# Four alternating layers on one core: PSUM pools of the linear-attention layer split by purpose, small loads and adds moved between engines, weight pieces requested in another order

## The chip, the core and the metric

The kernel runs on one core of a Trainium2 chip. The metric is the device time of one execution in microseconds. Before the change the median of four runs is 8587.26 us (8576.44 to 8593.6).

## What is computed

Four layers run one after the other on x (2048 tokens, 640 features, bf16): A, B, A, B, each as x + layer(layernorm(x)). Layer A is attention in 64 segments of 32 tokens, with 8 memory tokens ahead of each; the first 8 output rows of a segment are the memory of the next, so the segments are a chain. Layer B is linear attention with 32 heads of 20 features:

```
qkv = x @ wqkv                       # 640 -> 3 * 640, 32 heads of 20
pq, pk = q @ w_phi, k @ w_phi        # 20 x 20 for each head
phi_q = concat(softmax(pq), softmax(-pq)); phi_k likewise    # 40 features
kv = sum over s of phi_k * v;  z = sum over s of phi_k
o  = (phi_q @ kv) / (phi_q @ z + 1e-6)
y  = o @ wo
```

## The kernel before

`_layer_a` keeps Wq and Wo in SBUF (16 loads from ScalarE's queue, lines 77 to 82) and streams Wk and Wv anew for each segment: 8 pieces of 960 KB each, into rings of three buffers (`ringk`, `ringv`), requested on SyncE at line 147. A segment projects k and q in three thirds each, then v in three thirds (lines 165 to 169), and goes on to scores, softmax, the product with v and the output projection (lines 176 to 284).

`_layer_b` works in tiles of 128 tokens, 16 in all. Its stages are:

- Start-up: wqkv and wo on SyncE (lines 414 to 417), the 32 blocks of w_phi as 36 small loads on POOL's queue into `wphi_sb` (lines 425 and 427), x into `x_all` (line 472, POOL), layer norm (lines 479 to 489) and transposes into `xnT_all`.
- Key loop (lines 510 to 529): `proj_featT` makes k transposed (25 matmuls, line 504, copied by ScalarE at 506), then v (line 516, copied by VectorE at 518 to 522), then `phi_proj` (lines 447 to 451) and `phi_features` (lines 457 to 466: maximum and minimum, two exponentials on ScalarE, sum, reciprocal, product), which leaves the 40 features per head in `phik_all`.
- Sum over the keys (line 536): 512 matmuls into `kvp`, copied to `kv_sb`.
- Query loop (lines 543 to 583), for each tile: `proj_featT`, `phi_proj`, `phi_features`, 16 transposes (line 553) and a copy of 2048 columns (555), 32 small matmuls with `kv_sb` (560), the scaling by the denominator on VectorE (564 to 568), 5 transposes (572) and a copy (574), 10 matmuls with wo (578), the residual add on VectorE (581, 582) and the store from POOL's queue (583).

The PSUM tiles of projection, v, phi, transposed features, numerators and y all come from one pool, `psG`, with two buffers of two banks each; `phi_features` reads its input from there. SBUF tiles of the two loops come from `tw`, with two buffers for each tag. The framework sets the order of the instructions on each engine beforehand, from the dependences and the pools' buffers; on the chip every engine runs its list in that order, and a wait holds all that stands behind it.

Of the kernel before, what the change touches and what calls it, by code (L numbers as in the profile page):

```python
# [8 lines left out]
BF16 = mybir.dt.bfloat16  # L9
F32 = mybir.dt.float32  # L10
I32 = mybir.dt.int32
ALU = mybir.AluOpType
# [3 lines left out]
P = 128  # L16


def _layer_a(
# [10 lines left out]
    nc = tc.nc  # L30
    S, Dm = x_in.shape
    DC = Dm // P
# [15 lines left out]
    FPV = F // NPIECE_V  # L48
# [3 lines left out]
    ident = gctx["ident"]  # L52
# [4 lines left out]
    wk_v = wk.rearrange("(c p) h e -> p c (h e)", p=P)  # L57
    wv_v = wv.rearrange("(c p) h e -> p c (h e)", p=P)
# [3 lines left out]
    ringk = ctx.enter_context(tc.tile_pool(name="a_ringk", bufs=3))  # L62
    ringv = ctx.enter_context(tc.tile_pool(name="a_ringv", bufs=3))
# [11 lines left out]
    wo_sb = wres.tile([P, FB, Dm], BF16, name="wo_sb")  # L75
# [16 lines left out]
    for ti in range(NT):  # L92
# [7 lines left out]
        for c in range(nchk):  # L100
# [8 lines left out]
                                op0=ALU.subtract, op1=ALU.mult)  # L109
# [11 lines left out]
        for si in range(SPT):  # L121
            s = ti * SPT + si
# [17 lines left out]
            NPK = F // FPV  # L140
            R = 3

            def emit_pieces(wdram_v, ring, tagname, idxs):
                d = {}
                for pi in idxs:
                    pc = ring.tile([P, DC, FPV], BF16, name=f"{tagname}_piece", tag=tagname)
                    nc.sync.dma_start(out=pc[:], in_=wdram_v[:, :, pi * FPV:(pi + 1) * FPV])
# [158 lines left out]
def kernel(  # L306
# [15 lines left out]
    dbg_y: bass.AP | None = None,  # L322
):
    nc = tc.nc
# [9 lines left out]
    gctx = {}  # L334
# [43 lines left out]
def _layer_b(  # L378
# [16 lines left out]
    assert HB * DB == Dm and HB % 2 == 0 and HB * HS == 1024 and DB < HS and FF <= 64  # L395
    NT = S // P
    NPAIR = HB // 2
    HPB = 512 // HS
    eps_t = gctx["eps"]
# [20 lines left out]
    for h in range(HB):  # L420
        r0 = h * DB
        c = r0 // P
        p0 = r0 % P
        n1 = min(DB, P - p0)
        nc.gpsimd.dma_start(out=wphi_sb[p0:p0 + n1, c, h * HS:h * HS + DB], in_=wphi[h, 0:n1, :])
        if n1 < DB:
            nc.gpsimd.dma_start(out=wphi_sb[0:DB - n1, c + 1, h * HS:h * HS + DB], in_=wphi[h, n1:DB, :])

    interior = []
    straddle = []  # L430
    for c in range(DC):
        r_lo, r_hi = c * P, (c + 1) * P
        h_first = -(-r_lo // DB)
        h_last = r_hi // DB - 1
        lo = h_first
        while lo <= h_last:
            hi = min(h_last, (lo // HPB) * HPB + HPB - 1)
            interior.append((c, lo, hi))
            lo = hi + 1
        if r_hi < Dm and r_hi % DB != 0:  # L440
            straddle.append((r_hi // DB, c))

    def phi_proj(ps3, featT_sb):
        flat = ps3[:].rearrange("p h f -> p (h f)")
        for (c, h_lo, h_hi) in interior:
            a, b = h_lo * HS, h_hi * HS + DB
            nc.tensor.matmul(flat[:, a:b], lhsT=featT_sb[:, c, :], rhs=wphi_sb[:, c, a:b], start=True, stop=True)
        for (h, c) in straddle:
            a, b = h * HS, h * HS + DB
            nc.tensor.matmul(flat[:, a:b], lhsT=featT_sb[:, c, :], rhs=wphi_sb[:, c, a:b], start=True, stop=False)  # L450
            nc.tensor.matmul(flat[:, a:b], lhsT=featT_sb[:, c + 1, :], rhs=wphi_sb[:, c + 1, a:b], start=False, stop=True)

    def phi_features(ps3, out_phi):
        pf3 = ps3[:, :, 0:DB]
# [13 lines left out]
                                in1=sm[:].unsqueeze(3).to_broadcast([P, HB, 2, DB]), op=ALU.mult)  # L468

# [30 lines left out]
    def proj_featT(t, col0, dst_sb):  # L500
        ps = psG.tile([P, DC, P], F32, name="b_pT", tag="g")
        for fb in range(DC):
            for c in range(DC):
                nc.tensor.matmul(ps[:, fb, :], lhsT=wqkv_sb[:, c, col0 + fb * P:col0 + (fb + 1) * P],
                                 rhs=xnT_all[:, t * DC + c, :], start=(c == 0), stop=(c == DC - 1))
        nc.scalar.copy(out=dst_sb[:], in_=ps[:])

    hA = 512 // DB
    rem = 512 - hA * DB
    for t in range(NT):  # L510
        kT_sb = tw.tile([P, DC, P], BF16, name="b_kT", tag="featT")
        proj_featT(t, Dm, kT_sb)
        psv = psG.tile([P, 2, 512], F32, name="b_psv", tag="g")
        for c in range(DC):
            for part, (a, b) in enumerate(((0, 512), (512, Dm))):
                nc.tensor.matmul(psv[:, part, 0:b - a], lhsT=xnT_all[:, t * DC + c, :],
                                 rhs=wqkv_sb[:, c, 2 * Dm + a:2 * Dm + b], start=(c == 0), stop=(c == DC - 1))
        nc.vector.tensor_copy(out=v1_all[:, t, 0:hA, 0:DB], in_=psv[:, 0, 0:hA * DB].rearrange("p (h d) -> p h d", d=DB))
        if rem > 0:
            nc.vector.tensor_copy(out=v1_all[:, t, hA, 0:rem], in_=psv[:, 0, hA * DB:512])  # L520
            nc.vector.tensor_copy(out=v1_all[:, t, hA, rem:DB], in_=psv[:, 1, 0:DB - rem])
            nc.vector.tensor_copy(out=v1_all[:, t, hA + 1:HB, 0:DB],
                                  in_=psv[:, 1, DB - rem:Dm - 512].rearrange("p (h d) -> p h d", d=DB))
        else:
            nc.vector.tensor_copy(out=v1_all[:, t, hA:HB, 0:DB],
                                  in_=psv[:, 1, 0:Dm - 512].rearrange("p (h d) -> p h d", d=DB))
        psk = psG.tile([P, HB, HS], F32, name="b_psk", tag="g")
        phi_proj(psk, kT_sb)
        phi_features(psk, phik_all[:, t, :, :])
# [13 lines left out]
    for t in range(NT):  # L543
        qT_sb = tw.tile([P, DC, P], BF16, name="b_qT", tag="featT")
        proj_featT(t, 0, qT_sb)
        psq = psG.tile([P, HB, HS], F32, name="b_psq", tag="g")
        phi_proj(psq, qT_sb)
        phiq = tw.tile([P, NPAIR, 2, 64], BF16, name="b_phiq", tag="phiq")
        nc.vector.memset(phiq[:, :, :, FF:64], 0.0)
        phi_features(psq, phiq[:].rearrange("p j a f -> p (j a) f")[:, :, 0:FF])  # L550
        pqt = psG.tile([P, NPAIR, P], BF16, name="b_pqt", tag="g")
        for j in range(NPAIR):
            nc.tensor.transpose(out=pqt[:, j, :], in_=phiq[:, j, :, :].rearrange("p a f -> p (a f)"), identity=ident[:])  # L553
        phiqT = tw.tile([P, NPAIR, P], BF16, name="b_phiqT", tag="phiqT")
        nc.scalar.copy(out=phiqT[:], in_=pqt[:])  # L555
        psn = psG.tile([P, 2, NPAIR, HS], F32, name="b_psn", tag="g")
        for a in range(2):
            r0 = a * 64
            for j in range(NPAIR):
                nc.tensor.matmul(psn[:, a, j, 0:DB + 1], lhsT=phiqT[r0:r0 + FF, j, :],  # L560
                                 rhs=kv_sb[r0:r0 + FF, j, 0:DB + 1], start=True, stop=True)
        psn_ja = psn[:].rearrange("p a j s -> p j a s")
        rden = tw.tile([P, NPAIR, 2], F32, name="b_rden", tag="rden")
        nc.vector.tensor_scalar(out=rden[:].unsqueeze(3), in0=psn_ja[:, :, :, DB:DB + 1], scalar1=1e-6,
                                scalar2=None, op0=ALU.add)
        nc.vector.reciprocal(out=rden[:], in_=rden[:])
        o_sb = tw.tile([P, Dm], BF16, name="b_o", tag="o")
        nc.vector.tensor_tensor(out=o_sb[:].rearrange("p (j a d) -> p j a d", a=2, d=DB), in0=psn_ja[:, :, :, 0:DB],
                                in1=rden[:].unsqueeze(3).to_broadcast([P, NPAIR, 2, DB]), op=ALU.mult)
# [5 lines left out]
        psy = psG.tile([P, 2, 512], F32, name="b_psy", tag="g")  # L575
        for c in range(DC):
            for part, (a, b) in enumerate(((0, 512), (512, Dm))):
                nc.tensor.matmul(psy[:, part, 0:b - a], lhsT=oT_sb[:, c, :], rhs=wo_sb[:, c, a:b],  # L578
                                 start=(c == 0), stop=(c == DC - 1))
        xo = tw.tile([P, Dm], BF16, name="b_xo", tag="xo")  # L580
        nc.vector.tensor_tensor(out=xo[:, 0:512], in0=x_all[:, t, 0:512], in1=psy[:, 0, 0:512], op=ALU.add)
        nc.vector.tensor_tensor(out=xo[:, 512:Dm], in0=x_all[:, t, 512:Dm], in1=psy[:, 1, 0:Dm - 512], op=ALU.add)
# [36 lines left out]
```

## Time and profile before

| | |
|---|---|
| median of four runs | 8587.26 us |
| profiled execution | 8571.85 us |
| its span | 8570.1 us |
| busy share of PE, PEld, DVE, ACT, POOL | 69%, 62%, 28%, 22%, 1% |
| mean granted TensorE clock | 0.69 |

PE is TensorE's matmuls, PEld its weight loads, DVE is VectorE, ACT is ScalarE, POOL is GpSimd, SP is SyncE. In a row of the timeline stand start, length, engine, line and operation, output and inputs, count, and in brackets how long the engine had been idle and what released it. In a row of costs by line stand the busy time, the mean in ns of one instruction, and the idle time of the engine ahead of it with its releasers. The busy shares are of the whole span, in which layer A has about 87%; what an engine does in layer B is read from windows of that layer.

### The profile page before, as it was taken

The page shows a single profiled execution, that of the slowest core. Times are in us where ns is not written, and L with a number is a line of the kernel's source. Part 1 is how long each engine was busy: PE and PEld are TensorE (multiplying, and loading weights), DVE is VectorE, ACT ScalarE, POOL GpSimd, SP SyncE. Part 2 cuts the span into 40 slices and gives each one's busy share as a digit, 9 for nine tenths or more (in the row PEclk, how much of TensorE's full clock was granted, in tenths as well). Part 3 has the DMA queues.
Part 4 walks back from the last instruction along what each step waited for, and adds up shares of the span by engine and source line. Part 5 has one row for each costly group of instructions (what it writes and reads, how often), then busy time and mean ns, then how long its engine had stood idle before and what let it go on. Part 6 is the DMA issues. An engine that isn't in the chain of part 4 may idle for free.

```text
span 8570.1 us, 324610 instructions
## 1 busy us (share of the span) xinstructions
PE 5916.6 (69%) x156010; PEld 5344.3 (62%) x156010; DVE 2369.8 (28%) x4948; ACT 1854.7 (22%) x2568; POOL 108.4 (1%) x209
## 2 busy tenths in 40 slices
PE   5777777777777777765457777777777777777554
PEld 4666666666666666654346666666666666666543
DVE  2222222222222222235312222222222222222443
ACT  1222222222222222222212222222222222222222
POOL 0000000000000000010000000000000000000100
PEclk7777766766767676666666666667666766766766
DMA  8778778778877877840087787788778787778400
GB/s 306 271 274 281 271 271 286 274 272 279 283 266 275 281 267 272 281 162 6 8 305 271 275 284 271 272 286 284 266 273 289 264 282 270 274 273 280 150 6 8
DMA packets 1381604, 2093.24 MB, mean 244 GB/s; under 512 B 37808, under 2 KB 1376192, under 8 KB 1380288
## 3 DMA queue, kind: packets, MB, share of 16 engines
q1 hardware_dynamic: 1348736, 2019.95, 67.5%
q10 hardware_dynamic: 23040, 31.46, 1.1%
q8 instruction: 1220, 19.99, 1.0%
q0 software_dynamic: 8512, 21.06, 0.8%
q14 instruction: 96, 0.79, 0.0%
HBM read 2061.83 MB, written 10.49 MB: 242 GB/s over the span
## 4 chain that ended last, share of the span: by engine, by line
issue 43%; PE 7%; DVE 2%; DMA 2%; ACT 1%; POOL 0%; POOLq 0%; ACTq 0%
PE p L136 3%; DMA wk_piece<-in_A_Wk_dram 2%; PE y L283 1%; PE vstg L235 1%; DVE v_tok L238 1%; PE po L265 0%; DVE ssb L206 0%; ACT E L210 0%; DVE ssb L204 0%; DVE rmax L208 0%; PE ptp L219 0%; DMA wv_piece<-in_A_Wv_dram 0%; PE b_psy L578 0%; PE b_pqt L553 0%; ACT b_phiqT L555 0%
## 5 line engine op out<-in xcount | busy, mean ns | idle before, releaser
L136 PE MATMUL p<-hT,wv_piece 128*128 128x40 bf16 x30720 | 1120.2, 196 | 486.9 <-DMA wv_piece<-in_A_Wv_dram 362.6
L136 PEld LDWEIGHTS <-wv_piece 128*128 128x128 bf16 x30720 | 1024.8, 107 | 594.4 <-DMA wv_piece<-in_A_Wv_dram 404.7
L136 PE MATMUL p<-hT,wk_piece 128*128 128x40 bf16 x30720 | 1048.6, 188 | 351.4 <-DMA wk_piece<-in_A_Wk_dram 208.4
L136 PE MATMUL p<-hT,wq_sb 128*128 128x40 bf16 x30720 | 1031.5, 190 | 255.0 <-ACT qT_sb L138 122.7
L136 PEld LDWEIGHTS <-wk_piece 128*128 128x128 bf16 x30720 | 942.4, 101 | 387.8 <-DMA wk_piece<-in_A_Wk_dram 231.0
L136 PEld LDWEIGHTS <-wq_sb 128*128 128x128 bf16 x30720 | 969.7, 103 | 304.6 <-issue 294.5
L204 DVE SCALAR_TENSOR_TENSOR ssb<-sA,mask_a 40x640 f32<-40x640 f32 x256 | 210.5, 822 | 2999.4 <-PE sA L182 2995.5
L283 PE MATMUL y<-oT_sb,wo_sb 128*128 128x40 bf16 x30720 | 930.4, 191 | 3.3 <-issue 2.9
L283 PEld LDWEIGHTS <-wo_sb 128*128 128x128 bf16 x30720 | 915.7, 105 | 10.5 <-issue 4.5
L238 DVE COPY v_tok<-vstg 40x1024 bf16<-40x1024 bf16 x768 | 529.1, 689 | 1202.5 <-PE vstg L235 1190.3
L235 PE MATMUL vstg<-ident,vT_sb 128*40 128x128 bf16 x6144 | 700.8, 297 | 212.2 <-ACT vT_sb L138 100.0
L235 PEld LDWEIGHTS <-vT_sb 128*40 128x40 bf16 x6144 | 509.9, 137 | 275.2 <-ACT vT_sb L138 115.2
L138 ACT CAST kT_sb<-p 128x640 bf16<-128x640 f32 x384 | 265.8, 692 | 1641.8 <-PE p L136 1641.8
L138 ACT CAST qT_sb<-p 128x640 bf16<-128x640 f32 x384 | 265.3, 691 | 1352.0 <-PE p L136 1352.0
L265 PE MATMUL po<-PT_sb,v_tok 40*128 40x40 bf16 (+1 forms) x8192 | 335.6, 209 | 298.8 <-DVE v_tok L238 298.8
L265 PEld LDWEIGHTS <-v_tok 40*128 40x128 bf16 (+1 forms) x8192 | 268.0, 124 | 417.7 <-DVE v_tok L238 393.4
L138 ACT CAST vT_sb<-p 128x640 bf16<-128x640 f32 x384 | 265.8, 692 | 1144.4 <-PE p L136 1144.4
L269 ACT CAST oT_sb<-po 128x640 bf16<-128x640 f32 x384 | 265.7, 692 | 615.7 <-PE po L265 597.2
L292 DVE CAST hT<-y 128x8 bf16<-128x8 f32 x640 | 102.8, 161 | 1034.9 <-PE y L283 1034.9
L219 PE MATMUL ptp<-ident,Pn 40*40 40x40 bf16 x4096 | 183.8, 199 | 276.6 <-DVE Pn L213 276.6
L210 ACT ACTIVATE E<-ssb,nrmax 40x640 bf16<-40x640 f32 x256 | 211.2, 825 | 675.8 <-DVE nrmax L209 672.5
L219 PEld LDWEIGHTS <-Pn 40*40 40x40 bf16 x4096 | 154.6, 113 | 297.8 <-DVE Pn L213 291.5
(123 smaller groups left out, 3964.0 us busy)
## 6 DMA issues: line engine op xcount, KB each, us to landing
wk_piece<-in_A_Wk_dram SPq DMA_DIRECT2D x1024, 960.0 KB, 7.9
wv_piece<-in_A_Wv_dram SPq DMA_DIRECT2D x1024, 960.0 KB, 8.3
wq_sb<-in_A_Wq_dram ACTq DMA_DIRECT2D x16, 960.0 KB, 13.3
wo_sb<-in_A_Wo_dram ACTq DMA_DIRECT2D x16, 960.0 KB, 12.7
xscr<-xo_sb POOLq DMA_DIRECT2D x32, 160.0 KB, 2.1
x_all<-xscr POOLq DMA_DIRECT2D x32, 160.0 KB, 5.6
wqkv_sb<-in_B_wqkv_dram SPq DMA_DIRECT2D x6, 800.0 KB, 10.7
x_sb<-in_A_x_dram POOLq DMA_DIRECT2D x16, 160.0 KB, 2.6
```

Of the source, the lines that this page charges most:

```text
L136: nc.tensor.matmul(ps[:, bb, 0:L], lhsT=wb[:, c, :], rhs=hT[:, c, :], start=(c == 0), stop=(c == DC - 1))
L138: nc.scalar.copy(out=dst_sb[:, t3 * 16:(t3 + 1) * 16, :], in_=ps[:, :, 0:L])
L204: nc.vector.scalar_tensor_tensor(out=ssb4, in0=sA[rows, :, :, 0:L], scalar=scale, in1=mask4, op0=ALU.mult, op1=ALU.add)
L210: nc.scalar.activation(out=E[rows], in_=ssb[rows], func=ACT.Exp, bias=nrmax[rows], scale=1.0)
L219: nc.tensor.transpose(out=ptp[r0:r0 + L, g, hid, 0:L], in_=Pn[r0:r0 + L, hid, :], identity=ident[r0:r0 + L, r0:r0 + L])
L235: nc.tensor.transpose(out=stg[g * 64:g * 64 + L, jj, :], in_=vT_sb[:, jg, :], identity=ident[:])
L238: nc.vector.tensor_copy(out=v_tok[g * 64:g * 64 + L, st_i * STG:(st_i + 1) * STG, :], in_=stg[g * 64:g * 64 + L, :, :])
L265: nc.tensor.matmul(po[p0:p0 + sz, bb, 0:L], lhsT=v_tok[r0:r0 + L, jloc, c0:c0 + sz], rhs=PT_sb[r0:r0 + L, hid, :], start=True, stop=True)
L269: nc.scalar.copy(out=oT_sb[:, b_lo:b_lo + 16, :], in_=po[:, :, 0:L])
L283: nc.tensor.matmul(y_ap(c), lhsT=wo_sb[:, k, c * P:(c + 1) * P], rhs=oT_sb[:, k, :], start=(k == 0), stop=(k == FB - 1))
L292: nc.vector.tensor_copy(out=hT_next[:, c, 0:M], in_=y_ap(c)[:, 0:M])
```

## The change

In layer A the eight pieces of Wk are requested ahead of the eight of Wv in the code, where before the first three of each came first. In layer B:

- `psG` is replaced by pools for each purpose: `psP` (projection), `psQ` (phi), `psYV` (v and y), `psQT` (transposed features) with one bank each, `psN` (numerators) with two; `psT` goes from two buffers to one. Work that took two banks at once is done in parts: projection 4 + 1 blocks, phi in two halves of 16 heads, v in 512 + 128 columns one after the other, transposed features in two halves, numerators in four quarters, y in two halves of 320.
- phi is copied by ScalarE to a bf16 tile in SBUF (`pfsb`), and `phi_features` reads that.
- `tw` has three buffers.
- The 36 small loads of w_phi alternate between SyncE and ScalarE.
- The memset of `phiq` moves to GpSimd. y is copied by ScalarE to `ybf`, and GpSimd adds x to it.
- A flag `mimic_b` is passed that nothing reads.

```diff
-            kp = emit_pieces(wk_v, ringk, "wk", range(0, min(R, NPK)))
-            vp = emit_pieces(wv_v, ringv, "wv", range(0, min(R, NPK)))
-            kp.update(emit_pieces(wk_v, ringk, "wk", range(min(R, NPK), NPK)))
-            vp.update(emit_pieces(wv_v, ringv, "wv", range(min(R, NPK), NPK)))
+            kp = emit_pieces(wk_v, ringk, "wk", range(0, NPK))
+            vp = emit_pieces(wv_v, ringv, "wv", range(0, NPK))
...
-    tw = ctx.enter_context(tc.tile_pool(name="b_tw", bufs=2))
+    tw = ctx.enter_context(tc.tile_pool(name="b_tw", bufs=3))
...
-    psG = ctx.enter_context(tc.tile_pool(name="b_psG", bufs=2, space=bass.MemoryType.PSUM))
-    psT = ctx.enter_context(tc.tile_pool(name="b_psT", bufs=2, space=bass.MemoryType.PSUM))
+    psP = ctx.enter_context(tc.tile_pool(name="b_psP", bufs=1, space=bass.MemoryType.PSUM))
+    psQ = ctx.enter_context(tc.tile_pool(name="b_psQ", bufs=1, space=bass.MemoryType.PSUM))
+    psYV = ctx.enter_context(tc.tile_pool(name="b_psYV", bufs=1, space=bass.MemoryType.PSUM))
+    psQT = ctx.enter_context(tc.tile_pool(name="b_psQT", bufs=1, space=bass.MemoryType.PSUM))
+    psN = ctx.enter_context(tc.tile_pool(name="b_psN", bufs=2, space=bass.MemoryType.PSUM))
+    psT = ctx.enter_context(tc.tile_pool(name="b_psT", bufs=1, space=bass.MemoryType.PSUM))
...
-        nc.gpsimd.dma_start(out=wphi_sb[p0:p0 + n1, c, h * HS:h * HS + DB], in_=wphi[h, 0:n1, :])
+        eng = (nc.sync, nc.scalar)[h % 2]
+        eng.dma_start(out=wphi_sb[p0:p0 + n1, c, h * HS:h * HS + DB], in_=wphi[h, 0:n1, :])
...
+    def phi_proj(featT_sb, pfsb):
+        for half in range(2):
+            ps = psQ.tile([P, HH, HS], F32, name="b_psq", tag="q")
...
+            nc.scalar.copy(out=pfsb[:, half * HH:(half + 1) * HH, :], in_=ps[:, :, 0:DB])
...
-        nc.vector.memset(phiq[:, :, :, FF:64], 0.0)
+        nc.gpsimd.memset(phiq[:, :, :, FF:64], 0.0)
...
+        for jr in range(2):
+            pqt = psQT.tile([P, JH, P], BF16, name="b_pqt", tag="qt")
...
+            nc.scalar.copy(out=phiqT[:, jr * JH:(jr + 1) * JH, :], in_=pqt[:])
...
+        for jr in range(2):
+            for a in range(2):
...
+                nc.vector.tensor_scalar(out=rden[:].unsqueeze(2), in0=psn[:, :, DB:DB + 1], scalar1=1e-6,
+                                        scalar2=None, op0=ALU.add)
+                nc.vector.reciprocal(out=rden[:], in_=rden[:])
+                nc.vector.tensor_tensor(out=o4[:, jr * JH:(jr + 1) * JH, a, :], in0=psn[:, :, 0:DB],
+                                        in1=rden[:].unsqueeze(2).to_broadcast([P, JH, DB]), op=ALU.mult)
...
+            nc.scalar.copy(out=ybf[:, a:a + YR], in_=psy[:, 0:YR])
...
-        nc.vector.tensor_tensor(out=xo[:, 0:512], in0=x_all[:, t, 0:512], in1=psy[:, 0, 0:512], op=ALU.add)
-        nc.vector.tensor_tensor(out=xo[:, 512:Dm], in0=x_all[:, t, 512:Dm], in1=psy[:, 1, 0:Dm - 512], op=ALU.add)
+        nc.gpsimd.tensor_tensor(out=xo[:], in0=x_all[:, t, :], in1=ybf[:], op=ALU.add)
```

VectorE in the query loop before, one tile and the start of the next; the number behind a name tells one buffer's use from the next (`b_psn` numerators, `b_o` their scaled values, `b_psy` y, `b_psq` phi):

```order
L564 TENSOR_SCALAR b_rden_85452<-b_psn_85419 128x32
L566 RECIPROCAL b_rden_85452<-b_rden_85452 128x32
L568 TENSOR_TENSOR b_o_85455<-b_psn_85419,b_rden_85452 128x640
L581 TENSOR_TENSOR b_xo_85476<-x_all_82803,b_psy_85465 128x512
L582 TENSOR_TENSOR b_xo_85476<-x_all_82803,b_psy_85465 128x128
L457 TENSOR_REDUCE b_mx_85525<-b_psq_85508 128x1
L458 TENSOR_REDUCE b_mn_85526<-b_psq_85508 128x1
L459 TENSOR_SCALAR b_mx_85525<-b_mx_85525 128x1
L464 TENSOR_REDUCE b_sm_85533<-b_eph_85530 128x64
L465 RECIPROCAL b_sm_85533<-b_sm_85533 128x64
L466 TENSOR_TENSOR b_phiq_85523<-b_eph_85530,b_sm_85533 128x32x40
```

A tile's features (457 to 466) stand behind the last step of the tile before it. VectorE in the same loop now, in the same names (`b_pqsb` is the bf16 copy of phi); from one tile to the next the number of a name grows by 163:

```order
L592 TENSOR_TENSOR b_o_85844<-b_psn_85884,b_rden_85893 128x8x20
L473 TENSOR_SCALAR b_mx_86137<-b_mx_86137 128x1
L471 TENSOR_REDUCE b_mx_86300<-b_pqsb_86279 128x1
L472 TENSOR_REDUCE b_mn_86301<-b_pqsb_86279 128x1
L473 TENSOR_SCALAR b_mx_86300<-b_mx_86300 128x1
L478 TENSOR_REDUCE b_sm_86145<-b_eph_86142 128x64
L589 TENSOR_SCALAR b_rden_86017<-b_psn_86008 128x8
L589 TENSOR_SCALAR b_rden_86030<-b_psn_86021 128x8
L591 RECIPROCAL b_rden_86017<-b_rden_86017 128x8
L591 RECIPROCAL b_rden_86030<-b_rden_86030 128x8
L592 TENSOR_TENSOR b_o_86007<-b_psn_86008,b_rden_86017 128x8x20
L592 TENSOR_TENSOR b_o_86007<-b_psn_86021,b_rden_86030 128x8x20
```

Between the last quarter of one tile (`b_o_85844`) and the first of the next (`b_o_86007`) stand maxima and sums of the two tiles behind that (`b_mx_86137` and `b_mx_86300`).

SyncE in layer A, its rows word for word from both kernels: first before, from the first segment on,

```order
L147 DMA wk_piece<-in_A_Wk_dram 128x5x768 x3
L147 DMA wv_piece<-in_A_Wv_dram 128x5x768 x3
L147 DMA wk_piece<-in_A_Wk_dram 128x5x768 x6
L147 DMA wv_piece<-in_A_Wv_dram 128x5x768 x5
L147 DMA wk_piece<-in_A_Wk_dram 128x5x768 x2
```

and then now:

```order
L147 DMA wk_piece<-in_A_Wk_dram 128x5x768 x3
L147 DMA wv_piece<-in_A_Wv_dram 128x5x768 x3
L147 DMA wk_piece<-in_A_Wk_dram 128x5x768 x6
L147 DMA wv_piece<-in_A_Wv_dram 128x5x768 x5
L147 DMA wk_piece<-in_A_Wk_dram 128x5x768 x2
```

Nothing has moved; the last four rows, from three of v to two of k, go on with the same counts through the layer.

ScalarE at the head of the second layer A, before: the last copies of layer B, the weight loads, the transposed copies of the first tile,

```order
L555 COPY b_phiqT<-b_pqt 128x2048
L574 COPY b_oT<-b_otp 128x640
L79 DMA wq_sb<-in_A_Wq_dram 128x5x768 x8
L82 DMA wo_sb<-in_A_Wo_dram 128x6x640 x8
L114 COPY xnT_t<-tp_xn 128x640
```

and now:

```order
L79 DMA wq_sb<-in_A_Wq_dram 128x5x768 x8
L82 DMA wo_sb<-in_A_Wo_dram 128x6x640 x8
L105 ACT_TABLE_LOAD
L105 ACTIVATE rstd<-mv,eps_t 128x1
L106 ACT_TABLE_LOAD
L106 ACTIVATE rstd<-rstd 128x1
```

The rstd of the first tiles, which before stood among layer B's last tiles, stands behind the loads.

More of the change, by code (lines that the diff above doesn't have):

```diff
@@ L468, in phi_features, with proj_featT @@
                                 in1=sm[:].unsqueeze(3).to_broadcast([P, HB, 2, DB]), op=ALU.mult)
+    def proj_featT(t, col0, dst_sb):
+        fbs = list(range(DC))
+        for grp in (fbs[:4], fbs[4:]):
+            if not grp:
+                continue
+            ps = psP.tile([P, 4, P], F32, name="b_pT", tag="proj")
+            for i, fb in enumerate(grp):
+                for c in range(DC):
+                    nc.tensor.matmul(ps[:, i, :], lhsT=wqkv_sb[:, c, col0 + fb * P:col0 + (fb + 1) * P],
+                                     rhs=xnT_all[:, t * DC + c, :], start=(c == 0), stop=(c == DC - 1))
+            nc.scalar.copy(out=dst_sb[:, grp[0]:grp[-1] + 1, :], in_=ps[:, 0:len(grp), :])
     x_all = big.tile([P, NT, Dm], BF16, name="x_all")
@@ L498, in _layer_b @@
     phik_all = big.tile([P, NT, HB, FF], BF16, name="phik_all")
[L500 to L509, printed above, removed]
     for t in range(NT):
```

129 lines of the change are left out of this document (68 added, 61 removed).

## The prediction

> **What bounds the kernel now.** I read the windows of layer B first, then one tile of its query loop in the timeline, then the costs by line, then the queue of SyncE in layer A. The profiled execution took 8571.85 us, 1.75 us more than its span; the median of the four runs shown, 8587.26, is 15.4 above it. The runs lie 17 us apart, so 0.2% (17 us) is about what a measurement of this kernel can tell from no change.
>
> ```profile
> span 8570.1 us, 324610 instructions
> ```
>
> The windows cut the first layer B and what follows it into five stretches: start-up, key loop, sum over the keys, query loop, and the head of the second layer A. After the length come the busy times of PE, PEld, DVE, ACT and POOL with their instructions, the granted clock and the DMA share.
>
> ```profile
> 3768.80:3808.30 39.50, 0.91 (x5) 0.48 (x5) 18.79 (x63) 3.78 (x5) 27.21 (x53) 0.53 0.47 154
> 3808.30:3943.50 135.20, 83.27 (x918) 64.03 (x918) 101.64 (x178) 43.63 (x65) 0.52 (x1) 0.83 0.00 1
> 3943.50:3957.00 13.50, 12.76 (x476) 12.76 (x477) 4.28 (x5) 1.48 (x2) 0.00 (x0) 0.50 0.02 5
> 3957.00:4289.90 332.90, 144.84 (x1624) 108.29 (x1622) 121.10 (x192) 79.63 (x85) 9.20 (x17) 0.61 0.03 9
> 4289.90:4343.70 53.80, 0.82 (x10) 0.70 (x9) 1.45 (x6) 0.69 (x1) 0.54 (x1) 0.53 1.02 351
> ```
>
> The query loop is the long one: 332.9 us for 16 tiles, and no engine is busy for half of it (PE 44%, DVE 36%, ACT 24%). One tile in the timeline (start, length, engine, line, and in brackets the engine's idle time and its releaser) shows why.
>
> ```profile
> 4012.56 2.12 PE L504 MATMUL b_pT<-xnT_all,wqkv_sb 128*128 128x128 bf16 x25
> 4014.72 0.69 ACT L506 CAST b_qT<-b_pT 128x640 bf16<-128x640 f32 x1 [4.86 <-PE b_pT L504]
> 4016.23 0.82 DVE L457 TENSOR_REDUCE b_mx<-b_psq 128x1 f32<-128x640 f32 x1 [2.53 <-PE b_psq L451]
> 4019.45 1.49 DVE L464 TENSOR_REDUCE b_sm<-b_eph 128x64 f32<-128x1280 f32 x1 [1.61 <-ACT b_eph L462]
> 4023.11 1.89 PE L553 MATMUL b_pqt<-ident,b_phiq 128*128 128x128 bf16 x16 [6.92 <-DVE b_phiq L466]
> 4025.03 1.87 ACT L555 COPY b_phiqT<-b_pqt 128x2048 bf16<-128x2048 bf16 x1 [5.62 <-PE b_pqt L553]
> 4029.44 0.71 PE L572 MATMUL b_otp<-ident,b_o 128*128 128x128 bf16 x5 [1.53 <-DVE b_o L568]
> 4030.94 2.85 PE L578 MATMUL b_psy<-wo_sb,b_oT 128*128 128x512 bf16 x10 [0.78 <-ACT b_oT L574]
> 4033.58 1.87 PE L504 MATMUL b_pT<-xnT_all,wqkv_sb 128*128 128x128 bf16 x25
> ```
>
> Each engine waits for the one before it, and the next tile's projection starts only behind this tile's last matmul: 4012.56 to 4033.58 is 21.0 us per tile, one chain with nothing beside it. Five steps of a tile take their PSUM from the two buffers of one pool (psG), and the instruction order of before has no second tile in between. The second layer B has the same instructions.
>
> **The query loop, the term that decides.** The pool is split by purpose, so that tiles can overlap, and in the new order DVE makes features for up to three tiles ahead of the one whose output it scales. Then the fullest engine sets the period, so I sum each engine per tile. The costs by line end in busy time, mean ns, and idle time ahead; the first row is of the key loop alone, the others of the whole run.
>
> ```profile
> L464 DVE TENSOR_REDUCE b_sm<-b_eph 128x64 f32<-128x1280 f32 x16 | 23.8, 1486 | 25.9 <-ACT b_eph L462 25.9
> L466 DVE TENSOR_TENSOR b_phiq<-b_eph,b_sm 128x1280 bf16<-128x1280 f32 x32 | 47.7, 1492 | 1.1
> L465 DVE RECIPROCAL b_sm<-b_sm 128x64 f32<-128x64 f32 x64 | 35.4, 553 | 2.1
> L457 DVE TENSOR_REDUCE b_mx<-b_psq 128x1 f32<-128x640 f32 x32 | 26.4, 824 | 80.3 <-PE b_psq L451 80.3
> L459 DVE TENSOR_SCALAR b_mx<-b_mx 128x1 f32<-128x1 f32 x64 | 9.3, 145 | 0.0
> L568 DVE TENSOR_TENSOR b_o<-b_psn,b_rden 128x640 bf16<-128x640 f32 x32 | 26.4, 824 | 1.1
> L582 DVE TENSOR_TENSOR b_xo<-x_all,b_psy 128x128 bf16<-128x128 bf16 x32 | 9.0, 280 | 0.0
> L212 DVE RECIPROCAL rsum<-rsum 40x16 f32<-40x16 f32 x256 | 63.2, 247 | 7.9
> L555 ACT COPY b_phiqT<-b_pqt 128x2048 bf16<-128x2048 bf16 x32 | 59.7, 1866 | 191.0 <-PE b_pqt L553 191.0
> L506 ACT CAST b_qT<-b_pT 128x640 bf16<-128x640 f32 x32 | 22.1, 692 | 149.9 <-PE b_pT L504 149.9
> L461 ACT ACTIVATE b_eph<-b_psq,b_mx 128x640 f32<-128x640 f32 x32 | 25.4, 794 | 85.1 <-DVE b_mx L459 85.1
> ```
>
> DVE: maximum and minimum 2 x 0.82 (now from a bf16 copy; I take the same price), sign 0.15, sum 1.49, reciprocal 0.55, product 1.49, together 5.3. The scaling becomes four quarters: an add like the 0.15 us row, a reciprocal of 8 columns (0.2, under the 0.247 for 16), and a product of 160 columns, between 0.280 for 128 and 0.824 for 640, so 0.31. Four times 0.67 is 2.7. DVE loses the memset and the two residual adds. Its new sum is 8.0 us, against 121.1/16 = 7.6 now.
>
> ACT: 692 ns for 640 columns and 1866 for 2048 give 0.83 ns per column and 0.16 us fixed, so 0.59 for 512, 0.27 for 128, 0.43 for 320 and 1.01 for 1024. Query copies 0.85, phi copies 0.85, two exponentials 1.6, two transposed copies 2.0, output transpose 0.7, two copies of y 0.85: 6.9 us, against 79.63/16 = 5.0.
>
> PE: the count of matmuls is unchanged. Now 144.84/16 = 9.05 us at a mean clock of 0.61; at the key loop's clock of 0.83 it would be 9.05 x 0.61/0.83 = 6.7. The more continuous the work, the higher the clock in these two rows, and the new loop is more continuous than either. The Trainium skill says the same in "TensorE: Matmul & The Clock Gate" (Part 1: the HAM clock gate): half rate is the default, and a busy window of about 3.4 us lifts it. By that rule alone PE would run at full clock and take 9.05 x 0.61 = 5.5 us.
>
> So DVE's 8.0 is the longest. An engine in a chain of three, with single PSUM buffers between them, isn't busy all the time: the key loop reaches 101.64/135.20 = 75% with two shared buffers. I take 85%, 9.4 us per tile, 150 for the loop, **a saving of 183 us per layer**. Bounds: 98% gives 131 us (202 saved), 65% gives 197 us (136 saved). What fills and drains the pipeline lies partly under the 13.5 us of key sums, ahead of which the new order puts feature work of the first query tiles.
>
> **The key loop.** DVE waits 25.9 us there for the exponentials; the new order puts the next tile's maximum and the copies of v in between. I take 20 saved per layer, from 0 to 26.
>
> **The start-up.** POOL issues the last three loads of x behind 36 small loads of wphi.
>
> ```profile
> 3799.66 1.62 POOL L472 DMA_DIRECT2D x_all<-xscr  x3
> 3802.22 1.28 DVE L481 BATCH_NORM_STATS2 b_st<-x_all 128x6 f32<-128x320 bf16 x3 [12.52 <-DMA x_all<-xscr]
> 3805.14 1.28 ACT L484 ACT_TABLE_LOAD   x1 [34.37 <-DVE b_mv L482]
> wo_sb<-in_B_wo_dram SPq DMA_DIRECT2D x2, 800.0 KB, 16.3
> wphi_sb<-in_B_w_phi_dram POOLq DMA_DIRECT2D x56, 0.8 KB, 1.7
> ```
>
> With the small loads on SyncE and ScalarE, DVE goes straight on. The 12.52 us of waiting go, and some 3 us of memsets that DVE did ahead of it, at most 16 in all. But ScalarE now issues 18 of the loads ahead of the rstd that the layer waits for, each behind the landing of an earlier load, wo_sb's among them (16.3 us, so until about 3787); a dozen more at 1.7 us each, four in flight, end near 3794, and with the 3.2 us from table load to normalisation the first tile starts at 3797 instead of 3808, 11 saved. I take 13, from 16 saved to 10 lost (one load in flight only).
>
> **The head of the second layer A.** Layer B's larger pools move memory, and ScalarE's rstd of the first tile goes from ahead of the 16 weight loads to behind them. The first layer A already has that order:
>
> ```profile
> 30.63 22.52 ACTq L82 DMA_DIRECT2D wo_sb<-in_A_Wo_dram  x8
> 64.22 0.69 ACT L138 CAST kT_sb<-p 128x640 bf16<-128x640 f32 x1 [1.98 <-PE p L136]
> 4317.64 24.84 ACTq L82 DMA_DIRECT2D wo_sb<-in_A_Wo_dram  x8
> 4346.71 0.69 ACT L138 CAST kT_sb<-p 128x640 bf16<-128x640 f32 x1 [1.98 <-PE p L136]
> ```
>
> From the last weight issue to the first copy of k it is 64.22 - 53.15 = 11.1 us there and 4346.71 - 4342.48 = 4.2 here: 6.9 more. The first weight load also waits for the last store now, some 3 us. I take 10 lost, once, from 0 to 12.
>
> **The weight pieces of layer A** (k0 to k7, then v0 to v7 in the code): nothing. The queue of SyncE is the same in both orders, and the trace shows it as it runs:
>
> ```profile
> 2029.20 13.54 SPq L147 DMA_DIRECT2D wk_piece<-in_A_Wk_dram  x6
> 2047.54 11.04 SPq L147 DMA_DIRECT2D wv_piece<-in_A_Wv_dram  x5
> ```
>
> Six k pieces, then five of v: the scheduler had already put it so. The unused flag costs nothing either.
>
> **Sum:** 2 x (183 + 20 + 13) - 10 = 422 us saved; 8571.85 - 422 = 8150 beside the profiled execution, and 8587 - 422 = **8165 us** beside the median.
>
> **The rivals.** *PE becomes the bound*, with the clock left at 0.61: 9.05/0.85 = 10.6 us per tile, 170 per loop, 163 saved; 382 in all, 8205 us. For it speaks that the clock falls to 0.50 in the dense key sums; against it the key loop's 0.83. *POOL holds DVE up.* The residual add moves to POOL, which has no such row.
>
> ```profile
> L349 POOL IOTA mask_io<- 128x1024 int32 x1 | 1.0, 1022 | 0.0
> ```
>
> At that row's 1 ns per column 640 columns take 0.64 us, with two inputs perhaps 1.3, far under a tile's period; but if DVE stood still meanwhile, 32 tiles would cost 20 to 41 us, over 0.85 some 35, and the time would be 8200. The Trainium skill has a rule that speaks for this and against the edit: "GPSIMD Engine Reference" (section 8, key points) says the two share SBUF interfaces, with contention for DVE instructions that have two SBUF inputs, as the 1.49 us product has. By its measured add (section 3.1, 4497 ns for 2048 columns) my estimate is 1.4 us per tile. No run here shows that yet. *The overlap is partial*: waits on single buffers keep 15 us per tile, 240 per loop, 93 saved; 242 in all, 8345 us. The new order was laid out beforehand, and real latencies may fit it badly. *The tiles stay serial, slower than before*: if the next tile's steps stood behind this tile's y matmuls, the chain would grow by the phi copies (0.85), the split copy (0.16), the four scalings (1.3), the copies of y (0.85) and the add on POOL (0.7), less the two adds (0.97): 2.9 us x 32 = 93, less 66 of the other terms, plus 10, 8624 us. It decides if PE's order has no projection of a later tile ahead of y; it has. *The pieces of layer A do move*: then three v pieces of 960 KB, which now load during the attention, would load in the projections, at the 351 GB/s of the last window 2.8 us each, 8.4 x 128 segments = 1075 us, 9240 us. It decides from one v piece queued behind k7; the order has three v pieces ahead of the six.
>
> **Chances.** Forecast 0.60, PE 0.15, POOL 0.08, partial overlap 0.12, serial 0.03, pieces 0.02. All but the last two are faster: 0.94 faster, 0.01 the same, 0.05 slower. The low end takes the best bounds: 2 x (202 + 26 + 16) = 488 saved, 8099. The worst bounds of the forecast, 2 x (136 + 0 - 10) - 12 = 240 saved, give 8347, where the partial overlap lies. I give 8095 to 8330, which leaves out part of that case and the two slow ones.
>
> **What would show it.** Right: the query loop near 150 us with DVE busy around 85%, PE's clock over 0.8, start-up near 27 us, the key loop near 115, and the stretches of layer A as they were. The PE rival would show PE over 85% busy at a clock near 0.6; the POOL rival a product L480 longer than 1.49 us; partial overlap DVE under 60% busy, waiting for ACT or PE. The forecast is wrong if the query loop stays over 200 us, or if layer A changes by more than 20 us anywhere but at its head.

## The result, and the profile after

The changed kernel takes 8083.61 us (median of 8 runs, 8066.54 to 8088.83), the kernel before 8591.26 beside it: a ratio of 0.9407, 95% interval 0.9397 to 0.9416. That is 508 us less, where 422 were forecast, and 11 us under the low end of the range. The profiled execution has a span of 8064.8 us, 505.3 less than before.

These are the windows of the first layer B after the change, with the columns of the windows of before: start-up; first normalisation to the copy of the key sums; from there to the first weight load of layer A; from that to layer A's first matmul.

```profile
3768.42:3794.58 26.16, 0.91 (x5) 0.48 (x5) 17.78 (x61) 3.78 (x5) 11.17 (x20) 0.56 0.70 233
3794.58:3921.12 126.54, 101.75 (x1606) 81.45 (x1607) 113.88 (x195) 72.48 (x139) 0.00 (x0) 0.90 0.01 2
3921.12:4040.55 119.43, 99.60 (x1404) 75.67 (x1403) 96.92 (x271) 87.02 (x149) 40.64 (x44) 0.84 0.06 22
4040.55:4102.66 62.11, 1.47 (x16) 1.26 (x17) 3.58 (x11) 6.71 (x9) 2.17 (x4) 0.50 1.04 356
```

The query loop went from 333 to 119 us, key loop and key sums from 149 to 127, the start-up from 39.5 to 26.2; the head of layer A grew from 53 to 62. Measured between the same instructions, the first layer B is 249.6 us shorter and the second 256.0.

One stretch of the timeline of the changed kernel shows the overlap (L492 and L494 are the projection and its copy, L480 the product of the features, L586 the scaled sums, L592 their scaling, L575 the transposes of the features, L604 the output). A tile's output comes several steps behind its projection, so these rows are of different tiles.

```profile
3955.63 0.63 ACT L494 CAST b_qT<-b_pT 128x512 bf16<-128x512 f32 x1
3955.72 0.50 DVE L592 TENSOR_TENSOR b_o<-b_psn,b_rden 128x160 bf16<-128x160 f32 x2
3956.14 2.13 DVE L480 TENSOR_TENSOR b_phiq<-b_eph,b_sm 128x1280 bf16<-128x1280 f32 x1
3956.31 0.69 PE L492 MATMUL b_pT<-xnT_all,wqkv_sb 128*128 128x128 bf16 x5 [0.80 <-ACT b_qT L494]
3957.61 1.01 PE L492 MATMUL b_pT<-xnT_all,wqkv_sb 128*128 128x128 bf16 x8
3958.42 1.38 PE L604 MATMUL b_psy<-wo_sb,b_oT 128*128 128x320 bf16 x5
3959.64 0.61 PE L575 MATMUL b_pqt<-ident,b_phiq 128*128 128x128 bf16 x8
```

TensorE projects a later tile (3957.61) right ahead of the output of an earlier one (3958.42), while VectorE makes features of one tile between scalings of another. Before, the next projection came only behind y.

In the steady part of the query loop (8 tiles, by the scalings and products in it) the window and VectorE's costs by line are these: L471 and L472 are maximum and minimum, L473 the sign, L478 and L479 sum and reciprocal, L589 and L591 add and reciprocal of the scaling.

```profile
3943.82:4007.11 63.29, 54.87 (x831) 43.63 (x830) 56.51 (x146) 51.69 (x93) 23.35 (x26) 0.95 0.07 26
```

```profile
L480 DVE TENSOR_TENSOR b_phiq<-b_eph,b_sm 128x1280 bf16<-128x1280 f32 x8 | 14.5, 1813 | 0.0
L478 DVE TENSOR_REDUCE b_sm<-b_eph 128x64 f32<-128x1280 f32 x9 | 13.3, 1479 | 4.2 <-ACT b_eph L475 4.2
L592 DVE TENSOR_TENSOR b_o<-b_psn,b_rden 128x160 bf16<-128x160 f32 x32 | 8.8, 316 | 0.0
L471 DVE TENSOR_REDUCE b_mx<-b_pqsb 128x1 f32<-128x640 bf16 x8 | 6.5, 807 | 0.0
L472 DVE TENSOR_REDUCE b_mn<-b_pqsb 128x1 f32<-128x640 bf16 x8 | 6.3, 789 | 0.0
L479 DVE RECIPROCAL b_sm<-b_sm 128x64 f32<-128x64 f32 x9 | 4.9, 540 | 0.0
L591 DVE RECIPROCAL b_rden<-b_rden 128x8 f32<-128x8 f32 x32 | 4.8, 188 | 0.0
L589 DVE TENSOR_SCALAR b_rden<-b_psn 128x8 f32<-128x8 f32 x32 | 3.9, 153 | 2.5 <-PE b_psn L586 2.5
L473 DVE TENSOR_SCALAR b_mx<-b_mx 128x1 f32<-128x1 f32 x8 | 1.2, 144 | 0.0
```

The period is 63.29/8 = 7.9 us. By their mean lengths the rows of one tile come to 8.2 us, or to 7.9 with the product at the 1.49 us of before (some products are longer here, as the end of this document shows); 8.0 were forecast. But the window counts 56.51 us in which VectorE was busy at all, 7.1 per tile. The durations overlap. Consecutive rows of a full queue show how (the key loop):

```profile
3896.11 0.28 DVE L537 CAST v_all<-b_psv 128x120 bf16<-128x120 f32 x1
3896.30 0.55 DVE L479 RECIPROCAL b_sm<-b_sm 128x64 f32<-128x64 f32 x1
3896.76 0.11 DVE L541 CAST v_all<-b_psv 128x8 bf16<-128x8 f32 x1
3896.88 1.49 DVE L480 TENSOR_TENSOR phik_all<-b_eph,b_sm 128x1280 bf16<-128x1280 f32 x1
3898.29 0.81 DVE L472 TENSOR_REDUCE b_mn<-b_pksb 128x1 f32<-128x640 bf16 x1
3899.02 0.14 DVE L473 TENSOR_SCALAR b_mx<-b_mx 128x1 f32<-128x1 f32 x1
```

The row of 1.49 us is followed 1.41 us after its start, that of 0.81 after 0.73: each next instruction starts some 0.08 us inside the one before. In the serial tile of before, with a wait ahead of many instructions, that showed less. The Trainium skill gives a price for such a queue in "Vector Engine (DVE) Microarchitecture Reference" (section 5.2): 1.0417 ns per column and about 75 ns per instruction once the queue overlaps. My estimate from it is 1.41 us for 1280 columns and 0.74 for 640; the trace agrees with 1.41 and 0.73.

### The profile page after: what moved, and what is told of

It is laid out like the page before. It is cut to its first block, busy times and chain, and to the rows that moved or that the text cites. A ratio compares the mean times of both kernels' runs of the same rounds, so it can differ in the third digit from the quotient of the medians.

```text
span 8064.8 us, 325109 instructions
## 1 busy us (share of the span) xinstructions
PE 5835.5 (72%) x156010; PEld 5285.3 (66%) x156010; DVE 2338.5 (29%) x5140; ACT 1936.1 (24%) x2856; POOL 141.6 (2%) x201
## 5 line engine op out<-in xcount | busy, mean ns | idle before, releaser
L217 PE MATMUL ptp<-ident,Pn 40*40 40x40 bf16 x4096 | 184.1, 199 | 279.3 <-DVE Pn L211 279.3
```

The lines of the kernel that those rows point to most:

```text
L217: nc.tensor.transpose(out=ptp[r0:r0 + L, g, hid, 0:L], in_=Pn[r0:r0 + L, hid, :], identity=ident[r0:r0 + L, r0:r0 + L])
```

## The experiments

Layer A has the same instructions in every kernel here, in the same order but for the head of its second run, and it scatters: from one profiled execution to the next its first run ended at 3755 to 3777 us, and its second took 3690 to 3720 us behind its head. So beside each median stands the sum of the two stretches of layer B, from the first load of wqkv to the first weight load of layer A or to the end: 1049.6 us before, 544.0 after. "Over the changed kernel" is the plain difference of two medians. The kernel before, run beside each of them, took 8589 to 8591 us, but 8573 to 8574 beside the kernel with two rings, the two kernels with a bank moved and the doubled maximum. For these the plain difference is 12 to 19 us too small, and the ratio to before or layer B is the better measure.

**One ring in place of the split.**

```diff
-    psP ... psQ ... psYV ... psQT = ctx.enter_context(tc.tile_pool(..., bufs=1, ...))
-    psN = ctx.enter_context(tc.tile_pool(name="b_psN", bufs=2, space=bass.MemoryType.PSUM))
+    psG = ctx.enter_context(tc.tile_pool(name="b_psG", bufs=6, space=bass.MemoryType.PSUM))
```

> The changed kernel, but its five PSUM pools of layer B (6 banks: projection 1, features 1, value and output 1, transposed features 1, scaled sums 2) are one pool of 6 buffers, handed out in the order of the code. The number of banks is the same; only the split by purpose is undone. If the split is what lets the tiles overlap, a ring of 6 with 12 requests per tile reaches only half a tile ahead, DVE waits for PE and ACT in each tile, and the query loop goes from 120 us to 150 to 190: 60 to 140 us slower in all (two layers). If the number of small buffers alone does it, the time stays within 10 us of the changed kernel.

Measured: 8458.54 us (ratio to before 0.9844, 0.983 to 0.9859), 375 over the changed kernel; layer B 924.5. The window of its query loop, and its TensorE at the seam of two tiles (L600 is y, L488 the projection):

```profile
3910.40:4220.00 309.60, 151.95 (x1593) 113.33 (x1592) 111.97 (x284) 101.53 (x170) 40.54 (x45) 0.60 0.02 9
```

```profile
4054.68 2.85 PE L600 MATMUL b_psy<-wo_sb,b_oT 128*128 128x320 bf16 x10 [0.79 <-ACT b_oT L594]
4057.32 2.81 PE L488 MATMUL b_pT<-xnT_all,wqkv_sb 128*128 128x128 bf16 x25
...
4076.61 1.01 PE L600 MATMUL b_psy<-wo_sb,b_oT 128*128 128x320 bf16 x3
4077.41 2.87 PE L488 MATMUL b_pT<-xnT_all,wqkv_sb 128*128 128x128 bf16 x25
```

The tiles are serial again: projection behind y, 20.1 us from one to the next, with the same banks and the same small steps. The first expectation has the direction right and the size far too small. The ring is handed out in the order of the code, so a new tile's projection asks behind this tile's last steps, and the whole query-loop gain but 23 us is gone. By the count of the buffers the projection could have gone half a tile earlier; TensorE's order has it behind y all the same, and why is not shown. The key loop with the key sums stayed at 125.6, so its gain does not come from the split by purpose.

**Two rings, front and rest.**

```diff
+    psF = ctx.enter_context(tc.tile_pool(name="b_psF", bufs=2, ...))   # projection, features
+    psR = ctx.enter_context(tc.tile_pool(name="b_psR", bufs=4, ...))   # all later steps
```

> The changed kernel with the six PSUM banks of layer B as two rings: one of 2 buffers for the projection and the features, one of 4 for all that comes later in a tile (transposed features, scaled sums, output; the values of the key loop too). One ring of 6 for all cost 375 us; its trace shows every tile serial, 19.0 us. If what counts is that the first steps of the next tile do not queue for a bank behind the last steps of this one, two rings bring most of it back: layer B within 25 us of the changed kernel (544 us for both layers). If each step needs a bank of its own, layer B stays over 700 us.

Measured: 8099.74 us (0.944, 0.9423 to 0.9457), 16 over the changed kernel, or 28 by the ratios; layer B 564.6, 20.6 over it. So the split that matters is one: the next tile's first steps must not queue for a bank behind the last steps of this one.

**SBUF buffers: two in the changed kernel, three in the one before.**

```diff
-    tw = ctx.enter_context(tc.tile_pool(name="b_tw", bufs=3))
+    tw = ctx.enter_context(tc.tile_pool(name="b_tw", bufs=2))
```

> The changed kernel with two SBUF buffers per working tile of layer B in place of three. If the third buffer is what fills DVE (features of up to three tiles ahead), the query loop falls back to about 150 us, as forecast: 60 us slower in all. If the split of PSUM does it alone, within 15 us of the changed kernel.

Measured: 8093.61 us (0.942, 0.9406 to 0.9435), 10 over the changed kernel; layer B 559.6. The third buffer is worth 10 to 16 us, not 60.

> The kernel before with three SBUF buffers per working tile in place of two, PSUM as it was. If its two shared PSUM buffers hold the tiles in a chain, nothing: within 10 us of the kernel before, 21 us per tile of the query loop. If the SBUF buffers held the next tile back, the query loop falls under 250 us and the time by more than 160.

Measured: 8597.06 us (1.0006, 0.9996 to 1.0016): nothing, layer B 1050.6. But its second layer A had a head of 61.4 us against 53.2 in the kernel before: the larger SBUF pool alone is enough to lengthen that part.

**The small loads back on GpSimd.**

```diff
-        eng = (nc.sync, nc.scalar)[h % 2]
+        eng = nc.gpsimd
```

> The changed kernel with the 36 small loads of wphi back on the GpSimd queue, ahead of the last loads of x. If these loads made the start-up long, it goes from 26 us back to 39: 26 us slower in all. If the start-up was shortened by other things (memsets in another order), less than 6 us.

Measured: 8120.0 us (0.9451, 0.9437 to 0.9466), 36 over the changed kernel; layer B 573.7, 29.7 over it. Its start-up takes 38.1 us, and the old wait is back:

```profile
3803.89 1.62 POOL L498 DMA_DIRECT2D x_all<-xscr  x3
3806.39 1.28 DVE L507 BATCH_NORM_STATS2 b_st<-x_all 128x6 f32<-128x320 bf16 x3 [13.28 <-DMA x_all<-xscr]
```

The start-up term is what the queue order made it: 11.9 us in the first layer, 12.0 in the second. The other 6 us of layer B lie in the second query loop and are not explained.

**The residual add on VectorE.**

```diff
-        nc.gpsimd.tensor_tensor(out=xo[:], in0=x_all[:, t, :], in1=ybf[:], op=ALU.add)
+        nc.vector.tensor_tensor(out=xo[:], in0=x_all[:, t, :], in1=ybf[:], op=ALU.add)
```

> The changed kernel with the residual add of the query loop on VectorE, from the same SBUF copy of y, in place of GpSimd. In the profile of the changed kernel one of two products of the query features takes 2.15 us in place of 1.48 where GpSimd's add lies beside it. If VectorE bounds the query loop, it gains 0.33 us per tile there and pays for an add of 640 columns of two-byte data (0.4 to 1.0 us): 1 to 11 us slower per layer, 2 to 22 in all. If TensorE bounds it, no change within 4 us. If the collision costs more than the add, up to 6 us faster in all.

Measured: 8087.75 us (0.9415, 0.9402 to 0.9428), layer B 547.0: 4 and 3 us over the changed kernel, which is no difference. The add's and the product's durations there (minimum, median, maximum in ns):

```profile
L608 DVE TENSOR_TENSOR b_xo<-x_all,b_ybf x32: 440/492/494, 3929.5 to 8081.1; 128x640 bf16<-128x640 bf16 x32
...
L480 DVE TENSOR_TENSOR b_phiq<-b_eph,b_sm x32: 1427/1484/1493, 3902.6 to 8065.6; 128x1280 bf16<-128x1280 f32 x32
```

No product is longer than 1.49 us now, so the long ones of the changed kernel came from GpSimd's add; but the add costs VectorE 0.49 us per tile. The collision had lengthened 10 of the 32 products by 0.5 to 0.7 us, 6.4 us in all or 0.2 per tile.

**TensorE's share: eight transposes more.**

```diff
+                for rep in range(2 - jr):
                     nc.tensor.transpose(out=pqt[:, i, :], ...)
```

> The changed kernel with the first 8 of the 16 transposes of each query tile done twice (the second overwrites the first with the same values): 8 x 76 ns = 0.6 us of TensorE per tile. If TensorE (87% busy in the steady stretch) sets the period, 0.6/0.87 x 32 = 22 us slower in all; if VectorE does, TensorE's idle 13% (1.0 us per tile) takes it, within 6 us.

Measured: 8089.18 us (0.9423, 0.941 to 0.9436), 6 over the changed kernel; layer B 555.4, 11.4 over it. That is 0.36 us per tile of 0.6: between the two expectations. TensorE's idle time takes less than half of it, so it bounds the loop together with VectorE.

**VectorE's share: less and more.**

```diff
-        nc.vector.tensor_reduce(out=mx[:], in_=pf3, axis=AX.XY, op=ALU.max)
-        nc.vector.tensor_reduce(out=mn[:], in_=pf3, axis=AX.XY, op=ALU.min)
-        nc.vector.tensor_scalar(out=mx[:], in0=mx[:], scalar1=-1.0, ...)
+        nc.vector.tensor_reduce(out=mx[:], in_=pf3, axis=AX.XY, op=ALU.max, apply_absolute_value=True, negate=True)
```

> The changed kernel with one reduction of the largest absolute value, negated, as the shift of both exponentials, in place of maximum, minimum and sign (the softmax is the same in exact arithmetic). It takes away a row of 0.81 us and one of 0.15 us of VectorE from each tile of the key and the query loop. By the starts in the queue, which lie 0.73 and 0.06 us behind one another, they take 0.79 us. If VectorE bounds both loops, 64 x 0.79 = 50 us faster in all, or 61 if the full durations counted. If TensorE bounds the query loop, only the key loop gains: 25 us faster.

Measured: 8067.53 us (0.9395, 0.9382 to 0.9408); layer B 527.4, 16.6 under the changed kernel. Its windows, first normalisation to key sums, and query loop:

```profile
3788.83:3896.99 108.16, 89.48 (x1473) 73.79 (x1489) 93.46 (x153) 66.80 (x127) 0.00 (x0) 0.91 0.01 2
3896.99:4024.00 127.01, 105.90 (x1522) 81.78 (x1521) 91.21 (x250) 92.25 (x161) 41.33 (x44) 0.86 0.06 21
```

The first stretch lost 18.4 us, the query loop grew by 7.6. VectorE is busy 184.7 us in both together, 26.1 less than in the changed kernel (0.82 per tile, not the 0.95 of the rows), and 79% of the time instead of 86%; TensorE is at 83% of the query loop. In this kernel the features of two query tiles are done ahead of the key sums, in the changed kernel those of three, so some 4 us of VectorE's work moved from the first stretch to the second. Less VectorE work in the query loop did not shorten it even so: with VectorE lightened it no longer sets the pace there. What does is not shown. It is the fastest kernel of all, but by median 16 us under the changed one, with intervals that overlap.

```diff
+        for rep in range(2):
             nc.vector.tensor_reduce(out=mx[:], in_=pf3, axis=AX.XY, op=ALU.max)
```

> The changed kernel with the maximum of each tile's features reduced twice on VectorE, the second over the first: a row of 0.81 us whose successor starts 0.73 us behind it, in 16 key and 16 query tiles of each layer. In the steady key loop VectorE is busy 57.67 of 58.55 us, so each layer's stretch from the normalisation to the sums of the keys, which holds 16 key tiles and the features of 3 query tiles, grows by 19 x 0.73 = 14 us. If VectorE bounds the query loop as well, that grows by 13 x 0.73 = 9.5 per layer, 47 in all (layer B from 544 to 591). If it doesn't, it grows by less than 4 per layer, and layer B stays under 580.

Measured: 8142.58 us (0.9498, 0.9481 to 0.9514); layer B 606.8, 62.8 over the changed kernel. The same two windows:

```profile
3795.20:3932.30 137.10, 106.47 (x1616) 84.27 (x1617) 125.64 (x213) 73.11 (x141) 0.00 (x0) 0.89 0.01 2
3932.30:4069.40 137.10, 107.14 (x1394) 82.80 (x1393) 107.16 (x286) 87.76 (x147) 39.61 (x44) 0.81 0.06 19
```

More VectorE work costs its full price and some 16 us beyond the 47: VectorE does bound both loops then, busy 232.8 of 274.2 us, 85%. The surplus is not explained by its busy time, which grew by 22.0 us where the two stretches grew by 28.2; in this kernel the features of two query tiles are finished ahead of the key sums, in the changed kernel three.

**Banks moved by one.**

```diff
-    psP ... bufs=1        -    psN ... bufs=2
+    psP ... bufs=2        +    psN ... bufs=1
```

> The changed kernel with one bank moved: the projection gets two, the scaled sums get one. In the steady stretch PE waits 3.9 of 63 us for ACT to empty the projection's bank, and ACT 4.5 us for PE to fill it. If such handovers through one bank set the period of 7.9 us, the query loops gain up to 0.5 us per tile, 16 in all. If the engines' own work does (PE and DVE each 87% busy), or if the single bank of the scaled sums gives it back, within 6 us, or up to 20 slower.

Measured: 8160.72 us (0.9517, 0.9504 to 0.953), 77 over the changed kernel, or 95 by the ratios; layer B 626.3. The last expectation has the direction right, but its 20 us are far too small. What L589, the first step of the scaling, waited for over both layers (us, times):

```profile
  PE b_psn L586: 78.6, 81
```

In the changed kernel that wait is 15.5 us. The four quarters of a tile go to and fro between TensorE and VectorE; with one bank each trip is waited for.

> The changed kernel with the one reduction of the largest absolute value, and with one bank moved: value and output get two, the scaled sums get one. With the reduction alone DVE waited 16 us of a query loop for the scaled sums and ACT 12 for the output. If the output's single bank holds TensorE up, layer B falls below 520 us for both layers (527 with the reduction alone, 544 in the changed kernel); if the scaled sums need their two, it rises over 540.

Measured: 8123.04 us (0.9471, 0.9458 to 0.9484), layer B 597.0 (the diff is that of the one reduction, and psYV with two banks for psN's one). The scaled sums need their two, as the second expectation says: 70 us of layer B over the kernel with the one reduction, after 82 in the run above. Of the banks tried, the two of the scaled sums are the ones that must not be given away.

**The order of the weight pieces undone.**

```diff
-            kp = emit_pieces(wk_v, ringk, "wk", range(0, NPK))
-            vp = emit_pieces(wv_v, ringv, "wv", range(0, NPK))
+            kp = emit_pieces(wk_v, ringk, "wk", range(0, min(R, NPK)))
+            vp = emit_pieces(wv_v, ringv, "wv", range(0, min(R, NPK)))
+            ...
```

> The changed kernel with the weight pieces of layer A asked for in the old order of the code. If the scheduler had already put them in the same order, no change: within 8 us of the changed kernel, and the same rows of six k pieces and five v pieces. If the order of the code counts, more than 50 us either way.

Measured: 8090.35 us (0.942, 0.9408 to 0.9433), layer B 543.6. No difference.

## Why the prediction was wrong, step by step

**What failed: the sum of VectorE's row durations as its time per tile.** "DVE's 8.0 is the longest" added durations from a kernel in which instructions stood alone. The rows kept their lengths, 7.9 to 8.2 us per tile, but in a full queue they overlap to 56.51 for 8 tiles, 7.1 each. From the first normalisation to the first weight load of layer A it is 482.3 us before; less 183 and 20, the forecast is 279.3. In these the prediction's terms stand for 101.64 + 4.28 + 128 = 233.9 us of VectorE, 84%; measured are 210.80 in 245.97, 86%. The 23.1 us less, over 0.84, are 27.5 of the 33.3 us by which the first layer beat the forecast there, and the fuller queue is the rest. Counting each row only up to the start of the next, the 16 query tiles take 110.8 us, 6.9 each where the sum has 8.0: that is 17 of the 23. Another 5 were counted twice, since the windows of the key loop and the key sums before hold the features of the first query tile, which 16 x 8.0 has again. A row quoted for the start-up had shown the overlap: three BATCH_NORM_STATS2 in 1.28 us, 0.43 each, where one by itself has a row of 0.48.

So the bounds failed too. "98% gives 131 us" was no bound, since it rested on the same sum, and since VectorE does the features of three query tiles ahead of the key sums: the prediction mentioned that work and gave it no number. Two layers of 33.3 are 66.6 of the 83.3 us between 422 and 505.3. The rest is 0.6 of the start-ups, 6.4 of the second layer B, 1.1 of layer A's head, and 8.6 of layer A otherwise, which is within its scatter.

**What held.** That VectorE sets the pace at about 85%: doubling the maximum lengthened both loops and left it 85% busy. The 85% was chosen between 65 and 98, not worked out, so that it came out is partly luck. In the query loop VectorE does not set the pace alone, as the eight transposes show. TensorE was rightly close behind, closer than said: 54.87/8 = 6.9 us per tile at a clock of 0.95, and the kernel with one reduction looks as that rival said: VectorE lighter, TensorE at 83% and the loop no shorter. That the pool split decides was right, and the one ring shows it.

**Start-up:** 13 forecast, 13.3 and, by the return of the loads, 11.9 measured. ScalarE's queue limits it: the table load ahead of the rstd starts right behind the issue of its last small load. It does so by little, since VectorE's last statistics were ready at 3790.90. ScalarE's rows:

```profile
3772.05 14.70 ACTq L431 DMA_DIRECT2D wphi_sb<-in_B_w_phi_dram  x10
...
3791.42 1.28 ACT L510 ACT_TABLE_LOAD   x1 [21.06 <-DMA wphi_sb<-in_B_w_phi_dram]
```

**Head of the second layer A:** 10 forecast, 8.9 measured (53.2 to 62.1 us). The rstd stands behind the weight loads:

```profile
4068.94 25.20 ACTq L82 DMA_DIRECT2D wo_sb<-in_A_Wo_dram  x8
4094.53 1.28 ACT L105 ACT_TABLE_LOAD   x1 [55.48 <-issue]
```

Every kernel here but the one before has 61 to 63 us there, the kernel before with only its third buffer among them. The rest of that layer was 8.2 us shorter in the profiled execution, inside its scatter of 30. The second layer B gained 6.4 us more than the first, mostly behind its key sums; why was not tried.

**The key loop** gained its 20 us and more: 149 to 127 for loop and sums, and the features of three query tiles are in that, of one before. VectorE's 25.9 us of waiting for the exponentials are gone, as forecast; in the steady key loop of the changed kernel (58.55 us) its row reads:

```profile
L478 DVE TENSOR_REDUCE b_sm<-b_eph 128x64 f32<-128x1280 f32 x11 | 16.3, 1478 | 0.0
```

**Pieces of layer A:** nothing, shown by undoing it. The second segment of the second layer A reads as before:

```profile
4161.66 13.92 SPq L147 DMA_DIRECT2D wk_piece<-in_A_Wk_dram  x6
4182.02 10.72 SPq L147 DMA_DIRECT2D wv_piece<-in_A_Wv_dram  x5
```

**The rivals.** Partial overlap at 15 us per tile, and serial tiles, did not come; the one ring is what they would have looked like. GpSimd holding VectorE up did come, for 10 of the 32 products and 6.4 us in both layers, where the rival reckoned with 20 to 41.

## What to carry to other kernels

Durations taken from a serial stretch are too long for a queue that will be full: sum the distances of starts, and don't call a bound what rests on the sum of rows. When one PSUM ring serves all steps of a tile, the next tile's first step queues behind this tile's last; give the front of the tile buffers of its own before adding buffers anywhere, and keep two where a quarter goes to another engine and comes back. Here two engines came out close to each other, 56.51 and 54.87 us of 63.29: lightening one by 0.8 us per tile did not shorten that loop, and loading it further cost at least the full price.

## What was not expected of the hardware

GpSimd's add and VectorE's product of two SBUF inputs hardly run side by side; the later one nearly stands still. Rows of the changed kernel, first with GpSimd ahead, then with VectorE ahead:

```profile
3986.15 1.39 POOL L608 TENSOR_TENSOR b_xo<-x_all,b_ybf 128x640 bf16<-128x640 bf16 x1 [2.93 <-ACT b_ybf L606]
3986.74 2.15 DVE L480 TENSOR_TENSOR b_phiq<-b_eph,b_sm 128x1280 bf16<-128x1280 f32 x1
```

```profile
3931.85 1.48 DVE L480 TENSOR_TENSOR b_phiq<-b_eph,b_sm 128x1280 bf16<-128x1280 f32 x1
3932.53 2.06 POOL L608 TENSOR_TENSOR b_xo<-x_all,b_ybf 128x640 bf16<-128x640 bf16 x1 [3.30 <-ACT b_ybf L606]
```

The add ends at 3987.54, and the product, begun at 3986.74, takes 1.35 us from there; the other way round the product ends at 3933.33 and the add needs 1.26 more. Alone they take 1.48 and 1.39, so the later one got 0.13 us of its work done beside the other. The Trainium skill names the contention in "GPSIMD Engine Reference" (section 8) for VectorE instructions with two SBUF inputs; the trace agrees, and shows that it is a wait of up to 0.7 us each way. The estimate of 1.4 us for the add, from section 3.1 of that page of the Trainium skill, came out at 1.39.

TensorE's busy time did not follow the clock: 9.05 us per tile at a mean of 0.61 became 6.9 at 0.95, where the ratio of the clocks would give 5.8. By the rule that the prediction takes from the Trainium skill ("TensorE: Matmul & The Clock Gate", Part 1) its estimate was 5.5. Full clock came, 1.00 in a stretch of two tiles, but TensorE was busy for 13.71 us there, 6.9 per tile again. One reason is in the rows of the small matmuls with `kv_sb` (21 columns, 32 in a tile), first before, in 14 tiles, and then now, in 8:

```profile
L560 PE MATMUL b_psn<-kv_sb,b_phiqT 40*128 40x21 bf16 x448 | 13.3, 178 | 28.0 <-ACT b_phiqT L555 28.0
```

```profile
L586 PE MATMUL b_psn<-kv_sb,b_phiqT 40*128 40x21 bf16 x256 | 9.0, 171 | 1.3 <-DVE b_o L592 0.8
```

They take 0.95 us per tile before and 1.1 now: the higher clock did not shorten them. Idle time in the means is not a reason: over TensorE's busy time alone the clock is 0.58 before and 0.94 now. How the rest divides is not worked out.
